# Windowed attention and two feed-forward layers on one core: wider token groups, a shorter first attention, paired later attention, weights converted in place

## The chip, the cores and the metric

The program runs on one core of a Trainium2 chip. The metric is the device time of the program in microseconds (us), lower is better. TensorE does the matmuls (PE in the profile, PEld is its loading of weights), VectorE is DVE, ScalarE is ACT, GpSimd is POOL, and SP issues all DMAs.

## The reference, cut to what matters

All values are float32. There are 4 sequences of 576 tokens, 8 heads of 64, so 2304 tokens of 512 columns between the stages.

```python
# attention: a token sees itself and the 63 tokens before it
scores = scale * q @ k.T;  scores = where(0 <= rel < 64, scores, -1e9)
attn = exp(scores - max(scores)); attn = attn / (sum(attn) + 1e-9); x = attn @ v
# first layer: 512 -> 2048 -> 512
h = x @ w_in;  g = h * tanh(softplus(h));  x = g @ w_out
# second layer: 512 -> 1024 -> 512
h = x @ w_in2; sm = softmax(h); solu = h * sm
ln = (solu - mean(solu)) / sqrt(var(solu) + 1e-6) * g_ln
out = ln @ w_out2
```

## The kernel before, in words

Every matmul of the two layers is made of three: an operand is split into a high part `hi`, which holds its leading bits, and a rest `lo`, and hi x lo, lo x hi and hi x hi are added in PSUM.

**Weights.** They arrive as 64-bit words, two 32-bit halves to a value, in 48 pieces of 128 x 512 values (512 KB each). `convert` (L816) makes the steps of one piece. `c_load` (L304) fetches it into one of 3 `st` buffers; the first four go into a room of their own (`room_b`). `c_up` (L322) scales the upper halves into a new tile `wf`, on ACT (the first two pieces also on POOL). `c_low` (L332) scales the lower halves into a tile `wl`, on POOL. `c_bits` (L338, the instruction is L340) and `c_sign` (L344, L346) join them bit by bit in `wf`, on DVE. `c_hi` rounds `wf` to the high part (L263 on ACT, L267 on DVE) and `c_lo` subtracts it (L281 on POOL, L283 on DVE). 16 pieces each belong to `w_in` and `w_out`, 8 each to `w_in2` and `w_out2`.

**Attention.** It goes by blocks of 64 tokens, 36 in all, four matmuls of two heads each. The first group's 6 blocks come before anything else: scores in PSUM (L439, with the mask added by L442), maximum (L451), four exponentials with sums (L459), `a_norm` (L498, L499), the multiplication on POOL (L504), transposes (L518), a copy (L275), the product with v (L541), and its split into hi (`a_x`, L275) and lo (`a_xl`, L562), which lie in the group's tile `xt`. The other 30 blocks (`attend`, L913) are issued two at a time between the matmuls of the first layer. Each block has its own passes: scale and mask (L469), maximum (L475), subtraction (L481) and sum (L493) on DVE; only the exponentials (L489) of two blocks stand together, as they need another activation table than the first layer's function. Scores, transposes and products use the PSUM ring `a` of two buffers of one bank each; the first 6 blocks use the banks of `x2` and `h`.

**First layer.** There are 6 groups of 384 tokens. A tile of work is one group and one of 16 chunks of 128 columns of the 2048: `pe_m1` (L574, matmul L587, 12 of them), the activation (L597), rounding (L263 or L267) and rest (L283), then `pe_m2` (L621, 8 matmuls) and `pe_m2l` (L632, 4), which add into four banks `x2`. Groups 0 and 1 take chunks 0 to 7 in turn, write a partial sum to memory, and then chunks 8 to 15, where the partial sum is added; the other groups take all 16 at once. The m2 of a tile comes some tiles behind its m1 (`LAG`). At a group's end four copies (L657, L659) or sums (L647) go out to memory.

**Second layer.** 18 tiles of 128 tokens: load, split (L701), rest (L706 on POOL), 24 matmuls of 512 columns (L715), maximum (L722), exponential (L728), the product and statistics (L734 to L744), the power on POOL (L750), normalising (L756), transposes (L763), hi and lo (L769, L773), 24 matmuls (L788), copy (L795) and store.

**What sets the order.** Each function above is a step with a cost per engine and a due time. `Schedule.run` (L98) keeps a clock for every engine, takes the step that can start first (among those within `PATIENCE` the one with the earliest due time), picks the engine where `COSTS` names several, and issues the instructions in that order. So the order on each engine, and on SP for the DMAs, is fixed before the program runs, by modelled costs; on the chip semaphores hold an engine back where an input is late. Buffers are rings with a fixed number of places (`sch.run(dict(...))` at the end).

Of the kernel before, what the change touches and what calls it, by code (L numbers as in the profile page):

```python
# [26 lines left out]
LD = 2  # L27
CUT = 8
# [11 lines left out]
    "g_hi": {"dve": 0.28, "act": 0.42}, "g_lo": {"dve": 0.48},  # L40
    "x2": {"act": 0.39, "dve": 0.5},
# [15 lines left out]
G_AT = 10.0
K0_LATER = -3.349
W_STEP = 5.115
M4_LATER = -0.753  # L60
# [118 lines left out]
def attention_moe_solu(  # L179
# [27 lines left out]
    GROUPS = [384] * 6  # L207
# [3 lines left out]
    N0 = GROUPS[0] // BLK  # L211
    assert N0 <= NBB
    GMAX = max(GROUPS)

# [34 lines left out]
    st_p = actx.enter_context(tc.tile_pool(name="st", bufs=3))  # L249
# [8 lines left out]
    ps_a = tctx.enter_context(tc.tile_pool(name="ps_a", bufs=2, space=PSUM, side="right"))  # L258
# [62 lines left out]

    def c_up(e, p):  # L322
        p["wf"] = st_p.tile([P, 512], F32, tag="wf", name="wf")
        w = p["st"][:, :, 1].bitcast(F32)
        if e == "act":
            nc.scalar.activation(out=p["wf"], in_=w, func=ACTF.Copy, scale=2.0**-112)  # L326
        else:
            nc.gpsimd.tensor_scalar(
                out=p["wf"], in0=w, scalar1=2.0**-112, scalar2=0.0, op0=ALU.mult, op1=ALU.add
            )  # L330

    def c_low(p):  # L332
        p["wl"] = st_p.tile([P, 512], U32, tag="wl", name="wl", bufs=2)
        nc.gpsimd.tensor_scalar(  # L334
            out=p["wl"], in0=p["st"][:, :, 0], scalar1=0.9325 * 2.0**-29, scalar2=0.0, op0=ALU.mult, op1=ALU.add
        )

    def c_bits(p):  # L338
        wb = p["wf"].bitcast(U32)
        nc.vector.scalar_tensor_tensor(  # L340
            out=wb, in0=wb, scalar=3, in1=p["wl"], op0=ALU.logical_shift_left, op1=ALU.bitwise_or
        )

    def c_sign(p):  # L344
        wb = p["wf"].bitcast(U32)
        nc.vector.scalar_tensor_tensor(  # L346
            out=wb, in0=p["st"][:, :, 1], scalar=0x80000000, in1=wb, op0=ALU.bitwise_and, op1=ALU.bitwise_or
        )

# [32 lines left out]
    NI = NF * NG  # L382
    needs += [NI - NF + 4 + W_STEP * (n + 1) for n in range(2 * KD + NF2)]
# [21 lines left out]
    def open_q0():  # L405
        room["q"] = wpool.tile([P, N0 + 1, NP, P], F32, tag="w1", name="room_q")
        room["r"] = room["q"][:, N0, :2].bitcast(BF16)

# [25 lines left out]
    def a_qk(n):  # L434
        ps = ps_a.tile([P, NP, P], F32, tag="a", name="ps_s")
        r = room["r"]
        for p in range(NP):
            early = n < N0
            nc.tensor.matmul(out=ps[:, p, :], lhsT=qt[n][:, p, :], rhs=kt[n][:, p, :], start=True, stop=not early)  # L439
            if early:  # L440

                nc.tensor.matmul(  # L442
                    out=ps[:, p, :], lhsT=r[:, 0, :P], rhs=r[:, 0, P:] if n == 0 else r[:, 1, :P], start=False, stop=True
                )
# [11 lines left out]
    def a_exp0(n, ps=range(4)):  # L456
        s, nm, su, w = s_t[n]
        for p in ps:
            nc.scalar.activation(  # L459
                out=s[:, p], in_=w[:, p], func=ACTF.Exp, scale=scale, bias=nm[:, p:p + 1], accum_out=su[:, p:p + 1]  # L460
            )
        if 3 in ps:
            s_t[n] = s, nm, su

    def a_scale(n):
        ps = s_t[n]
        s = at_p.tile([P, NP, P], F32, tag="s", name="s", bufs=4)
        m = (mask_0 if n % NBB == 0 else mask_n).unsqueeze(1).to_broadcast([P, NP, P])
        nc.vector.scalar_tensor_tensor(out=s, in0=ps, scalar=scale, in1=m, op0=ALU.mult, op1=ALU.add)  # L469
        s_t[n] = s  # L470

    def a_max(n):
        s = s_t[n]
        nm = sm_p.tile([P, NP], F32, tag="nm", name="nm")
        nc.vector.tensor_reduce(out=nm, in_=s, axis=AX.X, op=ALU.max, negate=True)  # L475
        su = sm_p.tile([P, NP], F32, tag="su", name="su")
        s_t[n] = (s, nm, su)

    def a_sub(n):
# [34 lines left out]
    def a_tr(n):
        s = s_t.pop(n)
        ps = bank("x2", n, "ps_t", NP, P)
        for p in range(NP):
            nc.tensor.transpose(ps[:, p, :], s[:, p, :], ident)  # L518
        pt_t[n] = ps

    def a_pt(e, n):
        pt = at_p.tile([P, NP, P], F32, tag="pt", name="pt", bufs=2)
        copy(e, pt, pt_t[n])
        pt_t[n] = pt
# [10 lines left out]
    def a_pv(n):  # L535
        pt = pt_t.pop(n)
        ps = bank("h", n, "ps_o", NP, BLK)
        for p in range(NP):
            for h in range(2):
                r = slice(h * BLK, (h + 1) * BLK)  # L540
                nc.tensor.matmul(  # L541
                    out=ps[r, p, :],
                    lhsT=vt[n][:, (2 * p + h) * D:(2 * p + h + 1) * D],
                    rhs=pt[:, p, r],
                    start=True, stop=True,
                )
        x_t[n] = ps

    def a_x(e, n):
# [4 lines left out]
        hi = xt[j][:, 0, :, o:o + BLK]  # L554
        lo = xt[j][:, 1, :, o:o + BLK]
# [10 lines left out]

    its = [(j, f) for fs in (range(CUT), range(CUT, NF)) for j in range(2) for f in fs]
    its += [(j, f) for j in range(2, NG) for f in range(NF)]
    opens = {i for i, (j, f) in enumerate(its) if f == 0 or (f == CUT and j < 2)}
    closes = {i for i, (j, f) in enumerate(its) if f == NF - 1 or (f == CUT - 1 and j < 2)}  # L570
# [3 lines left out]
    def pe_m1(i):  # L574
        j, f = its[i]
        n = GROUPS[j]
# [4 lines left out]
        assert all(b in x_done for b in range(starts[j] // BLK, (starts[j] + GROUPS[j]) // BLK))  # L581
# [4 lines left out]
        for idx, (k, a, b) in enumerate(terms):  # L586
            nc.tensor.matmul(  # L587
                out=ps[:, :n], lhsT=w[:, a, k, fs], rhs=x[:, b, k, :n],
# [5 lines left out]
    def act_m(i):  # L594
        n = GROUPS[its[i][0]]
        c = m_p.tile([P, GMAX], F32, tag="mc", name="mc", bufs=3)
# [3 lines left out]
    def g_h(e, i):  # L600
        n = GROUPS[its[i][0]]
# [4 lines left out]
    def g_l(e, i):  # L606
        n = GROUPS[its[i][0]]
# [3 lines left out]
    def pe_m2(i):  # L611
        j, f = its[i]
        n = GROUPS[j]
# [5 lines left out]
        for m in range(KD):  # L619
            for a in (0, 1):  # L620
                nc.tensor.matmul(  # L621
                    out=acc[j][m][:, :n], lhsT=w[:, a, f % 4, m * P:(m + 1) * P], rhs=g[:, 0, :n],
# [3 lines left out]
    def pe_m2l(i):  # L626
        j, f = its[i]
        n = GROUPS[j]
        g = gt.pop(i)
        w = wt["w2", f // 4]  # L630
        for m in range(KD):
            nc.tensor.matmul(  # L632
                out=acc[j][m][:, :n], lhsT=w[:, 0, f % 4, m * P:(m + 1) * P], rhs=g[:, 1, :n],
# [9 lines left out]
    def evac_part(i, m):  # L643
        j, f = its[i]
# [7 lines left out]
    def evac_x2(e, i, m):  # L652
        j, f = its[i]
# [8 lines left out]
    def store_x2(i, m):  # L662
        j, f = its[i]
# [3 lines left out]
    with tc.manual_schedule():  # L667
        NI = len(its)
# [29 lines left out]
        def b_split(t):  # L698
            r = xr.pop(t)
            xs[t] = B["x"].tile([P, 2, KD, P], F32R, tag="xs", name="xs", bufs=3)  # L700
# [115 lines left out]
        def convert(p):  # L816
# [268 lines left out]
```

## Time and profile before

| | |
|---|---|
| median of 3 runs | 740.83 us (740.2 to 741.36) |
| profiled execution | 740.77 us |
| its span, first to last instruction | 739.0 us |
| mean granted TensorE clock | 0.988 |
| busy: PE, PEld, DVE, ACT, POOL | 706.6, 653.2, 425.4, 295.8, 156.3 us |
| moved by DMA | 70.45 MB |

Busy time is the length of all instructions of an engine without double counting. The matmul times are modelled at their end, so a batch's price is best read from the start of one batch to the start of the next. In a row of the groups, the mean is one instruction's length, and instructions that follow each other overlap by some tens of nanoseconds.

### The profile page before, as it was taken

What the parts mean: (1) busy time and instruction counts of PE and PEld (TensorE: products, weight loads), DVE (VectorE), ACT (ScalarE), POOL (GpSimd) and SP (SyncE); (2) the same over time, 40 slices, a digit from 0 to 9 for tenths busy, and PEclk for the clock granted to TensorE, in tenths of its full rate; (3) what the DMA queues carried; (4) which work ended last, traced back from release to release, by engine and by line L of the source; (5) the groups of instructions that cost most, each with busy time, mean ns of one, the idle gap of its engine ahead of it and who ended that gap; (6) DMA issues with size and microseconds to landing.
All of it is one profiled execution on the core that took longest, in us unless ns stands there. A gap on an engine that the chain in (4) does not pass through costs nothing.

```text
span 739.0 us, 11115 instructions
## 1 busy us (share of the span) xinstructions
PE 706.6 (96%) x4344; PEld 653.2 (88%) x4344; DVE 425.4 (58%) x734; ACT 295.8 (40%) x551; POOL 156.3 (21%) x176
## 2 busy tenths in 40 slices
PE   6797889699999999999999999999999999999998
PEld 5696789699999999999999999999888888888886
DVE  3999999955645334424434412676575646464642
ACT  4665435454454345334434433345432323232221
POOL 3556644421111011011101110331122111121000
PEclk9899999899999999999999999999999999999999
DMA  8645565652622201302222011331111111111001
GB/s 299 243 155 196 163 213 173 192 178 98 192 83 100 86 30 58 129 29 75 69 88 70 1 44 58 114 114 58 59 43 57 43 43 43 43 44 43 29 16 43
DMA packets 42916, 70.45 MB, mean 95 GB/s; under 512 B 3312, under 2 KB 27376, under 8 KB 42864
## 3 DMA queue, kind: packets, MB, share of 16 engines
q1 hardware_dynamic: 42864, 69.75, 28.6%
q8 instruction: 34, 0.56, 0.3%
q14 instruction: 18, 0.15, 0.1%
HBM read 58.72 MB, written 11.01 MB: 94 GB/s over the span
## 4 chain that ended last, share of the span: by engine, by line
PE 85%; DVE 10%; issue 2%; ACT 1%; DMA 1%; POOL 0%; SPq 0%; DVEq 0%; ACTq 0%; POOLq 0%
PE ps_h L587 24%; PE x L621 16%; PE h L715 14%; PE po L788 13%; PE x L632 8%; PE ps_s L439 4%; DVE wf L346 3%; DVE wf L340 3%; PE pt L763 2%; PE ps_o L541 2%; PE ps_t L518 2%; DVE g L283 1%; DVE w L267 1%; DMA room_q<-qk 0%; DVE su L493 0%
## 5 line engine op out<-in xcount | busy, mean ns | idle before, releaser
L587 PE MATMUL ps_h<-xt,w 128*128 128x384 f32 x1152 | 221.5, 341 | 5.6 <-POOL w L281 2.0
L587 PEld LDWEIGHTS ps_h<-xt,w 128*128 128x128 f32 x1152 | 204.5, 191 | 8.3 <-POOL w L281 2.8
L621 PE MATMUL x<-g,w 128*128 128x384 f32 x768 | 153.5, 340 | 9.4 <-ACT xs L657 6.2
L621 PEld LDWEIGHTS x<-g,w 128*128 128x128 f32 x768 | 134.9, 190 | 12.0 <-ACT xs L657 6.9
L283 DVE SCALAR_TENSOR_TENSOR g<-mc,g 128x384 fp32r<-128x384 f32 x96 | 69.8, 728 | 109.2 <-ACT g L263 108.5
L597 ACT ACTIVATE mc<-ps_h 128x384 f32<-128x384 f32 x96 | 47.0, 490 | 154.9 <-PE ps_h L587 154.6
L715 PE MATMUL h<-w,xs 128*128 128x512 f32 x432 | 104.2, 396 | 0.4 <-DVE y L734 0.4
L788 PE MATMUL po<-w,lz 128*128 128x512 f32 x432 | 102.3, 393 | 0.0
L715 PEld LDWEIGHTS h<-w,xs 128*128 128x128 f32 x432 | 80.8, 188 | 19.6 <-PE x L632 0.7
L504 POOL TENSOR_TENSOR s<-s,rs 128x512 f32<-128x512 f32 x36 | 40.6, 1145 | 257.3 <-DVE rs L498 109.7
L788 PEld LDWEIGHTS po<-w,lz 128*128 128x128 f32 x432 | 80.0, 188 | 16.4
L632 PE MATMUL x<-g,w 128*128 128x384 f32 x384 | 84.1, 340 | 0.0
L632 PEld LDWEIGHTS x<-g,w 128*128 128x128 f32 x384 | 67.6, 189 | 0.7
L334 POOL TENSOR_SCALAR wl<-st 128x512 uint32<-128x512 uint32 x44 | 37.6, 855 | 63.5 <-DMA st<-w_in 20.1
L722 DVE TENSOR_REDUCE nm<-h 128x1 f32<-128x1024 f32 x18 | 22.0, 1224 | 49.1 <-PE h L715 49.1
L263 ACT ACTIVATE g<-mc 128x384 fp32r<-128x384 f32 x87 | 45.8, 526 | 4.9 <-PE x L632 2.2
L326 ACT ACTIVATE wf<-st 128x512 f32<-128x512 f32 x44 | 29.3, 672 | 45.3 <-DMA st<-w_in 21.0
L706 POOL TENSOR_TENSOR xs<-xr,xs 128x512 fp32r<-128x512 f32 x18 | 23.3, 1294 | 95.2 <-ACT xs L701 95.2
L281 POOL TENSOR_TENSOR w<-wf,w 128x512 fp32r<-128x512 f32 x22 | 33.1, 1510 | 43.9 <-DVE w L267 40.3
L346 DVE SCALAR_TENSOR_TENSOR wf<-st,wf 128x512 uint32<-128x512 uint32 x44 | 40.5, 921 | 1.2
L340 DVE SCALAR_TENSOR_TENSOR wf<-wf,wl 128x512 uint32<-128x512 uint32 x48 | 40.8, 851 | 0.1
L701 ACT ACTIVATE xs<-xr 128x512 fp32r<-128x512 f32 x18 | 11.4, 632 | 62.9 <-PE h L715 46.9
(75 smaller groups left out, 671.9 us busy)
## 6 DMA issues: line engine op xcount, KB each, us to landing
qk<-qk SPq DMA_DIRECT2D x30, 512.0 KB, 4.4
st<-w_out SPq DMA_DIRECT2D x24, 512.0 KB, 3.6
st<-w_in SPq DMA_DIRECT2D x20, 512.0 KB, 3.8
v<-v SPq DMA_DIRECT2D x30, 256.0 KB, 2.8
x2d<-xs SPq DMA_DIRECT2D x24, 192.0 KB, 2.1
xr<-x2d SPq DMA_DIRECT2D x18, 256.0 KB, 3.1
out<-o SPq DMA_DIRECT2D x18, 256.0 KB, 2.0
room_b<-w_in SPq DMA_DIRECT2D x4, 512.0 KB, 7.8
```

Source lines behind the costliest of these rows:

```text
L263: nc.scalar.activation(out=hi, in_=x, func=ACTF.Copy, scale=1.0 if g is None else g)
L283: nc.vector.scalar_tensor_tensor(out=lo, in0=x, scalar=1.0 if g is None else g, in1=hi.bitcast(F32), op0=ALU.mult, op1=ALU.subtract)
L334: nc.gpsimd.tensor_scalar(out=p["wl"], in0=p["st"][:, :, 0], scalar1=0.9325 * 2.0**-29, scalar2=0.0, op0=ALU.mult, op1=ALU.add)
L340: nc.vector.scalar_tensor_tensor(out=wb, in0=wb, scalar=3, in1=p["wl"], op0=ALU.logical_shift_left, op1=ALU.bitwise_or)
L346: nc.vector.scalar_tensor_tensor(out=wb, in0=p["st"][:, :, 1], scalar=0x80000000, in1=wb, op0=ALU.bitwise_and, op1=ALU.bitwise_or)
L504: nc.gpsimd.tensor_tensor(out=s, in0=s, in1=rs.to_broadcast([P, NP, P]), op=ALU.mult)
L587: nc.tensor.matmul(out=ps[:, :n], lhsT=w[:, a, k, fs], rhs=x[:, b, k, :n], start=(idx == 0), stop=(idx == len(terms) - 1),)
L597: nc.scalar.activation(out=c[:, :n], in_=ht.pop(i)[:, :n], func=ACTF.Mish)
L621: nc.tensor.matmul(out=acc[j][m][:, :n], lhsT=w[:, a, f % 4, m * P:(m + 1) * P], rhs=g[:, 0, :n], start=(i in opens and a == 0), stop=False,)
L632: nc.tensor.matmul(out=acc[j][m][:, :n], lhsT=w[:, 0, f % 4, m * P:(m + 1) * P], rhs=g[:, 1, :n], start=False, stop=i in closes,)
L715: nc.tensor.matmul(out=h2[t][:, c, :], lhsT=x[:, a, k, :], rhs=wt["w3", c][:, b, k, :], start=(idx == 0), stop=(idx == len(terms) - 1),)
L788: nc.tensor.matmul(out=po[t], lhsT=lz[:, a, f, :], rhs=wt["w4", f // 4][:, b, f % 4, :], start=(c == 0 and idx == 0), stop=(c == 2 and idx ...
```

## The change: what it does

- The groups are 512, 512, 512, 384 and 384 tokens. The first four chunks of group 0 are done in two halves of 256 tokens, first all four of tokens 0 to 255, then of 256 to 511. There are 84 tiles: 8 of 256, 44 of 512, 32 of 384.
- Only 4 blocks, half a group, come before the first layer. Their scores lie in the `x2` banks, their exponentials in a spare part of the q room. The 28 others come in 14 pairs; a pair is one tile of 1024 columns for each pass (L465 to L520 before), and the ring `a` has one buffer of two banks. The transposed values are copied back over the exponentials in two halves. The multiplication may go to POOL or DVE.
- `c_up` and `c_low` write in place, into the staged piece; both run on ACT (the lower half of the first two pieces on POOL, the upper on either). Bits and sign are joined in the lower halves. `c_hi` runs on ACT, `c_lo` on DVE; the tiles `wf` and `wl` are gone, and there are 4 staging buffers.
- The activation's tile has 2 places instead of 3, the second layer's split input 2 instead of 3.
- Due times and modelled costs are new; positions are counted in time (`pos`), not in tiles.

```diff
 COSTS = {
-    "up0": {"act": 0.57, "pool": 0.846}, "up": {"act": 0.57},
-    "pt0": {"act": 0.5}, "x0": {"act": 0.29}, "pt": {"act": 0.5}, "x": {"act": 0.29},
-    "w0_hi": {"dve": 0.36, "act": 0.51}, "w0_lo": {"dve": 0.63, "pool": 1.5},
-    "w_hi": {"act": 0.51, "dve": 0.36}, "w_lo": {"dve": 0.63, "pool": 1.5},
+    "up0": {"act": 0.58, "pool": 0.7}, "up": {"act": 0.58},
+    "pt0": {"act": 0.5, "dve": 0.68}, "x0": {"act": 0.29}, "pt": {"act": 0.5}, "x": {"act": 0.5},
+    "low0": {"pool": 0.83}, "low": {"act": 0.58},
+    "w0_hi": {"dve": 0.43, "act": 0.54}, "w0_lo": {"dve": 0.69},
+    "w_hi": {"act": 0.54}, "w_lo": {"dve": 0.69},
...
+    "mul0": {"pool": 1.05, "dve": 0.69}, "mul": {"pool": 2.2, "dve": 1.23},
...
-    GROUPS = [384] * 6
+    GROUPS = [512, 512, 512, 384, 384]
...
-    N0 = GROUPS[0] // BLK
+    N0 = GROUPS[0] // BLK // 2
...
-    st_p = actx.enter_context(tc.tile_pool(name="st", bufs=3))
+    st_p = actx.enter_context(tc.tile_pool(name="st", bufs=4))
...
-    ps_a = tctx.enter_context(tc.tile_pool(name="ps_a", bufs=2, space=PSUM, side="right"))
+    ps_a = tctx.enter_context(tc.tile_pool(name="ps_a", bufs=1, space=PSUM, side="right"))
...
     def c_up(e, p):
-        p["wf"] = st_p.tile([P, 512], F32, tag="wf", name="wf")
         w = p["st"][:, :, 1].bitcast(F32)
         if e == "act":
-            nc.scalar.activation(out=p["wf"], in_=w, func=ACTF.Copy, scale=2.0**-112)
+            nc.scalar.activation(out=w, in_=w, func=ACTF.Copy, scale=2.0**-112)
...
+    def c_low(e, p):
+        w = p["st"][:, :, 0]
+        if e == "act":
+            nc.scalar.activation(out=w, in_=w, func=ACTF.Copy, scale=0.9325 * 2.0**-29)
...
+        lw, uw = p["st"][:, :, 0], p["st"][:, :, 1]
         nc.vector.scalar_tensor_tensor(
-            out=wb, in0=wb, scalar=3, in1=p["wl"], op0=ALU.logical_shift_left, op1=ALU.bitwise_or
+            out=lw, in0=uw, scalar=3, in1=lw, op0=ALU.logical_shift_left, op1=ALU.bitwise_or
         )
...
+    n = GROUPS[0] // 2
+    its = [(0, f, o, o + n) for o in (0, n) for f in range(HALF)]
+    its += [(0, f, 0, 2 * n) for f in range(HALF, CUT)]
+    its += [(1, f, 0, GROUPS[1]) for f in range(CUT)]
+    its += [(j, f, 0, GROUPS[j]) for j in range(2) for f in range(CUT, NF)]
+    its += [(j, f, 0, GROUPS[j]) for j in range(2, NG) for f in range(NF)]
...
     def a_scale(n):
         ps = s_t[n]
-        s = at_p.tile([P, NP, P], F32, tag="s", name="s", bufs=4)
+        s = at_p.tile([P, 2 * NP, P], F32, tag="s2", name="s", bufs=2)
...
+            qk = step(dict(pe=1.75), t + offs[0], a_qk, n, after=lks + pv_last[-2:-1], new=[S], uses=ks + [S])
+            sc = step(dict(dve=1.23), t + offs[1], a_scale, n, after=[qk, masks], new=[s], uses=[S, s])
+            mx = step(dict(dve=1.2), t + offs[2], a_max, n, after=[sc], new=[nm], uses=[s, nm])
...
+                su = step(dict(dve=1.23), t + offs[3], a_sub, n, after=[mx], uses=[s, nm])
+                ex = step(dict(act=1.03 + 2.66), t + offs[4], a_exp, n, after=[su], uses=[s])
+                sm = step(dict(dve=1.2), t + offs[5], a_sum, n, after=[ex], uses=[s])
...
+            mu = step(COSTS["mul"], t + offs[6], a_mul, n, after=[r], uses=[s, rs])
+            tr = step(dict(pe=0.87), t + offs[7], a_tr, n, after=[mu] + pv_last[-1:], new=[T], uses=[s, T])
+            c0 = step(COSTS["pt"], t + offs[8], a_pt, n, 0, after=[tr], uses=[T, s])
+            c1 = step(COSTS["pt"], t + offs[8], a_pt, n, 1, after=[tr, c0], uses=[T, s])
...
-            w1=4, w2=4, st=3, wf=3, wl=2, qk=LD, v=LD, a=2, s=4, nm=4, rs=4, pt=2, x2=4, h=2, xt=2, mc=3,
-            g=LAG, xs=4, bxr=1, bxs=3, b0=1, b1=1, bnm=4, bsu=4, by=2, bst=4, bt=1, blz=2, bo=2, bot=2,
+            w1=4, w2=4, st=4, qk=LD, v=LD, a=1, s=3, nm=4, rs=4, s2=2, nm2=4, rs2=4, x2=4, h=2, xt=2, mc=2,
+            g=LAG, xs=4, bxr=1, bxs=2, b0=1, b1=1, bnm=4, bsu=4, by=2, bst=4, bt=1, blz=2, bo=2, bot=2,
```

## Rows read from the trace of the kernel before

**Rows 1.** Page, busy tenths in 40 slices of 18.5 us.
```profile
PE   6797889699999999999999999999999999999998
...
DVE  3999999955645334424434412676575646464642
```

**Rows 2.** Busy us (instructions) by stage; then clock, DMA share, GB/s.
```profile
0.00:20.00 20.00, 13.19 (x107) 11.22 (x108) 8.32 (x21) 10.39 (x41) 7.97 (x21) 1.00 0.91 305
...
32.96:155.00 122.04, 105.32 (x639) 98.83 (x640) 117.62 (x167) 58.45 (x103) 62.37 (x56) 0.94 0.55 178
...
155.00:515.40 360.40, 360.40 (x2468) 355.73 (x2467) 163.63 (x303) 154.38 (x268) 44.61 (x42) 1.00 0.25 81
...
515.40:739.00 223.60, 219.57 (x1032) 180.93 (x1031) 123.66 (x222) 64.43 (x114) 33.54 (x51) 1.00 0.13 42
```

**Rows 3.** Chain of waits in order of time: start, length, what.
```profile
102.82 2.08 PE ps_h L587 x12
...
106.98 2.08 PE ps_h L587 x12
...
150.83 1.78 PE ps_s L439 x16
...
568.12 5.60 PE h L715 x24
574.59 5.48 PE po L788 x24
```

**Rows 4.** Timeline of PE: start, length, instructions, idle time before and its releaser.
```profile
140.50 1.65 PE L621 MATMUL x<-g,w 128*128 128x384 f32 x4 [4.41 <-ACT xs L657]
...
179.68 1.03 PE L518 MATMUL ps_t<-ident,s 128*128 128x128 f32 x8
...
180.47 1.65 PE L621 MATMUL x<-g,w 128*128 128x384 f32 x8
...
183.86 0.69 PE L541 MATMUL ps_o<-pt,v 128*64 128x64 f32 x16
```

**Rows 5.** Timeline of DVE, the fourth and the sixth block's L562.
```profile
26.70 0.42 DVE L562 TENSOR_TENSOR xt<-ps_o,xt 128x256 fp32r<-128x256 f32 x1
...
32.48 0.42 DVE L562 TENSOR_TENSOR xt<-ps_o,xt 128x256 fp32r<-128x256 f32 x1 [0.59 <-ACT xt L275]
```

**Rows 6.** Groups by line from 32.96 to 155 us: busy, mean, idle before.
```profile
L346 DVE SCALAR_TENSOR_TENSOR wf<-st,wf 128x512 uint32<-128x512 uint32 x31 | 30.8, 993 | 0.8
```

**Rows 7.** Groups by line of DVE, whole span.
```profile
L283 DVE SCALAR_TENSOR_TENSOR g<-mc,g 128x384 fp32r<-128x384 f32 x96 | 69.8, 728 | 109.2 <-ACT g L263 108.5
...
L722 DVE TENSOR_REDUCE nm<-h 128x1 f32<-128x1024 f32 x18 | 22.0, 1224 | 49.1 <-PE h L715 49.1
L734 DVE TENSOR_TENSOR y<-h,y 128x1024 f32<-128x1024 f32 x18 | 21.9, 1215 | 2.0 <-ACT y L728 2.0
...
L499 DVE RECIPROCAL rs<-rs 128x4 f32<-128x4 f32 x36 | 6.4, 178 | 1.2
...
L346 DVE SCALAR_TENSOR_TENSOR wf<-room_b,wf 128x512 uint32<-128x512 uint32 x4 | 2.7, 686 | 0.1
```

**Rows 8.** Groups by line of ACT, whole span.
```profile
L597 ACT ACTIVATE mc<-ps_h 128x384 f32<-128x384 f32 x96 | 47.0, 490 | 154.9 <-PE ps_h L587 154.6
...
L326 ACT ACTIVATE wf<-st 128x512 f32<-128x512 f32 x44 | 29.3, 672 | 45.3 <-DMA st<-w_in 21.0 <-DMA st<-w_out 19.4 <-DVE g L283 2.4
...
L275 ACT ACTIVATE pt<-ps_t 128x512 f32<-128x512 f32 x36 | 20.2, 596 | 9.9 <-PE ps_t L518 9.9
L728 ACT ACTIVATE y<-h,nm 128x1024 f32<-128x1024 f32 x18 | 20.2, 1122 | 8.2 <-DVE nm L722 8.2
...
L263 ACT ACTIVATE w<-wf 128x512 fp32r<-128x512 f32 x7 | 4.4, 634 | 4.5 <-DVE wf L346 4.5
```

**Rows 9.** Timeline of ACT around one switch of tables.
```profile
52.52 1.28 ACT L489 ACT_TABLE_LOAD   x1
53.82 1.15 ACT L489 ACTIVATE s<-s 128x512 f32<-128x512 f32 x2
```

More of the change, by code (lines that the diff above doesn't have):

```diff
@@ L434, in a_qk @@
     def a_qk(n):
[L435 to L444, printed above, removed]
+        early = n < N0
+        ns = (n,) if early else (n, n + 1)
+        if early:
+            ps = ps_x2.tile([P, NP, P], F32, tag="x2", name="ps_s")
+        else:
+            ps = ps_a.tile([P, 2 * NP, P], F32, tag="a", name="ps_s")
+        r = room["r"] if early else None
+        for c, m in enumerate(ns):
+            for p in range(NP):
+                o = ps[:, c * NP + p, :]
+                nc.tensor.matmul(out=o, lhsT=qt[m][:, p, :], rhs=kt[m][:, p, :], start=True, stop=not early)
+                if early:
+                    nc.tensor.matmul(
+                        out=o, lhsT=r[:, 0, :P], rhs=r[:, 0, P:] if n == 0 else r[:, 1, :P], start=False, stop=True
+                    )
         s_t[n] = ps
@@ L536, in a_pv @@
         pt = pt_t.pop(n)
[L537 to L546, printed above, removed]
+        if n < N0:
+            ps, ns = ps_h.tile([P, NP, BLK], F32, tag="h", name="ps_o"), (n,)
+        else:
+            ps, ns = ps_a.tile([P, NP, 2 * BLK], F32, tag="a", name="ps_o"), (n, n + 1)
+        for c, m in enumerate(ns):
+            for p in range(NP):
+                for h in range(2):
+                    r = slice(h * BLK, (h + 1) * BLK)
+                    nc.tensor.matmul(
+                        out=ps[r, p, c * BLK:(c + 1) * BLK],
+                        lhsT=vt[m][:, (2 * p + h) * D:(2 * p + h + 1) * D],
+                        rhs=pt[:, c * NP + p, r],
+                        start=True, stop=True,
+                    )
         x_t[n] = ps
@@ L580, in pe_m1 @@
         assert ("w1", 0, f) in split_done
-        assert all(b in x_done for b in range(starts[j] // BLK, (starts[j] + GROUPS[j]) // BLK))
+        assert all(b in x_done for b in range((starts[j] + a0) // BLK, (starts[j] + a1) // BLK))
         w = wt["w1", f // 4]
@@ L890, in values @@
[L890 to L901 removed]
+            w, pt = bufs
@@ L902, in values @@
+            pv = step(dict(pe=0.648 * len(cps)), t + offs[0], a_pv, n, after=cps, new=[O], uses=[pt, O] + w)
             new = []
@@ L926, in mish @@
         def mish(i):
-            j, f = its[i]
-            k = GROUPS[j] / 384
+            j, f, a0, a1 = its[i]
+            k = (a1 - a0) / 384
+            pe = pe_of(i)
             h, mc, g = (Buf(x) for x in ("x2" if i in H_X2 else "h", "mc", "g"))
-            o = [i + x for x in MISH_AT]
+            o = [pos[i] + x for x in MISH_AT]
             m1 = step(
-                dict(pe=2.081 * k), o[0], pe_m1, i, after=x_of[j] + [split_of["w1", 0, f]], new=[h],
+                dict(pe=pe / 2), o[0], pe_m1, i, after=list({id(x_of[n]): x_of[n] for n in range((starts[j] + a0) // BLK, (starts[j] + a1) // BLK)}.values()) + [split_of["w1", 0, f]] + ([m1_of[i - 1]] if i else []), new=[h],
@@ L938, in mish @@
+            gl = step(COSTS["g_lo" if a1 - a0 > 256 else "g_lo0"], o[3], g_l, i, after=[gh], uses=[mc, g])
             new = []
```

382 lines of the change are left out of this document (201 added, 181 removed).

## The prediction, made before the result was known

> **What bounds the kernel now.** I read the 40 slices first, then a table of stages, then the chain of waits. The slices [rows 1] show two regimes: up to slice 9 (about 150 us) DVE stands at 9 nearly throughout and PE at 5 to 9; from then on PE stands at 9 to the last slice and DVE mostly at 2 to 7. The stages say it in numbers [rows 2]. From 32.96 (first matmul of the feed-forward) to 155 us DVE is busy 117.62 of 122.04 us and PE 105.32; from 155 to 515.4 PE is busy 360.40 of 360.40; from 515.4 to the end 219.57 of 223.60. So the opening is DVE's and the rest is TensorE's.
>
> The chain [rows 3] gives TensorE's prices. One column tile of 384 tokens is 24 matmuls: 12 of m1, 8 of m2 and 4 of m2l, from 102.82 to 106.98 = 4.16 us (0.173 us each). A 512-wide batch of 24 takes 5.60 us (L715) or 5.48 (L788). A pair of attention blocks takes 1.78 for the scores, 0.79 for the transposes (from 179.68 to 180.47) and twice 0.69 for the values [rows 3, 4]: 3.9 us.
>
> These terms give the span back. First m1 at 32.96; 96 tiles x 4.16 = 399.4; the 30 blocks that remain = 15 pairs x 3.9 = 58.5; last part 739.0 - 515.4 = 223.6. Together 714.5; the span is 739.0, so 24.5 us are lost to waits and to the half clock after them. All of it lies before 155 us, since behind that PE is always busy. The profiled execution took 740.77 us, 1.77 over its span, and the median of the runs is 740.83: the sum below is made on the span, and 1.8 are added.
>
> **The change, part by part.**
>
> *Wider groups.* After: 8 tiles of 256 tokens, 12 + 32 = 44 of 512 and 32 of 384. For a 512 tile I take m1 at L715's price and m2 at L788's: (5.60 + 5.48)/2 = 5.54 us. A 256 tile has no row; on the line through 4.16 and 5.54 it is 2.78. Sum: 44 x 5.54 + 8 x 2.78 + 32 x 4.16 = 243.8 + 22.2 + 133.1 = 399.1 us, against 399.4. The width itself gives nothing: the same columns cross the array, and the small price per matmul that is saved is lost to the halves and to the 512 price. Ends: 5.48 and 5.60 for the 512 tile move the sum by 2.6 us either way; a 256 tile at 4.16 (no gain from being shorter) adds 11 us, one at 24 x 0.111 = 2.67 (the 128-wide score matmuls, 1.78/16) takes off 0.9. The line is kept, since the 128-wide row lies below it too.
>
> *Four blocks, not six, before the first m1.* The subtraction that ends a block's share of x is L562. It starts at 26.70 for the fourth block and at 32.48 for the sixth [rows 5]; m1 follows 0.06 us after its end. Left as it is, m1 would start at 27.1 us instead of 32.96. Five loads of 256 KB also go (two of q, one of k, two of v); the first 20 us move 305 GB/s [rows 2], so 1.31 MB are 4.3 us of the queue. Ends 22.8 and 27.1 (above: 31, if the in-place conversion comes late); I take 25.0. The two blocks move into the 28 that run beside the matmuls: 14 pairs x 3.9 = 54.6, which is 3.9 us less PE time after the start.
>
> *Conversion in place.* Each of 48 pieces is two scalings, two bit operations, hi and lo. Before, POOL did one scaling and part of the lo's, and DVE part of the hi's. After, ACT has both scalings and nearly all hi's, DVE the bit operations and lo's, POOL two pieces. What DVE wins is in the rows: L346 costs 0.993 us in the opening, beside POOL, and 0.686 on the staged pieces [rows 6, 7]. With POOL nearly gone from conversion I take 0.69 for each of three operations, 2.07 us a piece. The writes now step over every second word; reads of that form cost ACT 0.672 (L326) [rows 8], and I take the same for the writes (ends: 0.634, a dense one (L263), and double). The four staging buffers hold a piece until its lo is done; four pieces in flight against one needed every 5 us leave room.
>
> *Later attention in pairs.* DVE: four passes over 1024 columns at 1.22 (L722, L734), two tiny ones like L499 at 0.18, and a subtraction of 512 columns, 0.69 as L346: 5.9 us a pair. ACT: two table loads of 1.28, one exponential of 1024 at 1.12 (L728), three 512-wide copies at 0.60 (L275): 5.5 us [rows 7 to 9]. The multiplication may stand on POOL or, at 1.22, on DVE.
>
> The load of L489 lasts 1.28 us and the exponential starts 1.30 us after the load's start, so here nothing stands between them [rows 9]; a switch is costed at the load alone. The Trainium skill, page "ScalarE: Activation LUTs", section "What ACT_TABLE_LOAD costs", speaks against that: it puts every switch of sets at 2.66 us, since a drain of 1.38 follows the load, and by it the twelve switches of the opening would cost ACT an estimated 16 us more. Our row shows no such drain.
>
> *The new opening.* It reaches to the first tile of group 1, the 13th. By then these must be done: 16 pieces, 6 pairs (group 0's second half and group 1) and 12 tiles.
> - PE without a wait: 25.0 + 8 x 2.78 + 4 x 5.54 + 6 x 3.9 = 93 us.
> - DVE: 8.3 for the first blocks (its busy time in the first 20 us) + 16 x 2.07 + 6 x 5.9 + 12 x 0.73 (L283) = 86 us [rows 2, 7].
> - ACT: 10.4 + 16 x (2 x 0.672 + 0.634) + 6 x 5.5 + 12 x 2 x 0.49 (L597, and as much for a rounding) = 87 us [rows 2, 8].
>
> Before, DVE alone was the limit and was packed to 96%. Now two engines carry nearly the same load and every pair and piece passes from one to the other, so I take 90% packing from 8 us on: 8 + 87/0.9 = 105. PE then waits 12 us; with 2 for the half clock after waits, S = 14. The end of the opening is what counts: an m1 earlier than 25 only lengthens the wait. Ends: 96% gives 99 and S = 6, with nothing for the clock; 75% gives 124 and S = 33; the six muls on DVE (93 us) give 111 and S = 20. Behind the opening, DVE needs some 16 x 2.07 + 4 x 5.9 + 24 x 0.73 = 74 us over 24 tiles x 5.54 + 4 x 3.9 = 149 us of PE, so the conversion of the second half of the weights, which before still held PE up to 143 us (a wait of 4.41 us at 140.50 [rows 4]), is covered.
>
> *The rest.* The last part keeps its instructions; with two input buffers instead of three there are still 12 us between the end of one L715 batch and the need for the next but one, against a load, split and subtraction of some 5 us. I cost it at 0 (ends: -1 and +4).
>
> Sum: 25.0 + 399.1 + 54.6 + 14 + 223.6 = 716.3 of span, 718.1 us of time; before minus after is 8.0 (start) + 0.3 + 3.9 + 10.5 (waits) = 22.7.
>
> **Rivals.**
> - *The two engines pack as well as DVE did alone* (S = 6), and the 512 tile costs 5.48: 718.1 - 8 - 2.6 = 707 us. For it: ACT is busy only 58.45 of 122.04 us in the old opening, so load moves to an engine that was half free. Against: a pair is one chain over four engines, and each of its links is twice as long as a block's.
> - *ACT and DVE hand each other the wait* (75%, S = 33): 737 us. For it: ACT's order is fixed, and a copy out of PSUM that PE needs can now stand behind three conversions (2 us) or two table loads with an exponential (3.7 us). Against: DVE was in the same place for PE before, and its 96% left no such holes.
> - *A table switch costs its length once more*, 1.28 us on ACT for each of twelve: 8 + (87 + 15)/0.9 = 122, S = 31, 735 us. The Trainium skill's page named above is for it; the row of L489 [rows 9] is against it.
> - *One PSUM tile for all later attention: slower.* The ring of two one-bank buffers becomes one of two banks, which scores, transposes and values of a pair use in turn. If the planner's order leaves nothing to put between, PE stands through the scaling pass (1.22) and two copies (1.20) of each pair: 2.4 x 14 = 34 us, 752. It decides from 1.6 us a pair (22.7/14). Against: with two buffers PE waited in none of the 12 pairs after 155 us, and a pair has some 22 us there (four tiles of 5.54).
> - *It does not do what it says*: halves cost what 384 does (+8 with the 5.48), m1 starts at 31 (+6) and PE waits as before (S = 22): 740, no change.
>
> **How the numbers follow.** Forecast (710 to 728) 0.47, well packed 0.18, hand-over 0.18, table switch 0.02, PSUM slower 0.12, no change 0.03. The time is the forecast's, 718. The range, 703 to 738, takes in the first three cases with 4 us below 707, and leaves out the last two. A measurement here tells 0.2% (1.5 us) from no change: faster 0.85, same 0.03, slower 0.12.
>
> **What would show it.** First m1 matmul at 23 to 27 us; 12 m1 of 512 columns in 2.7 to 2.8 us; DVE and ACT both above 85% busy from the start to about 105 us and below 60% after; bit operations at 0.69; last part of 223 us. The forecast is wrong if PE has repeated gaps of 1 to 2 us in front of transposes or values after the opening, if the wide tiles cost over 5.8 us, or if the first m1 comes after 30 us.

## The result and the profile after

The changed kernel takes 720.98 us (median, 720.77 to 722.02), the kernel before beside it 740.52 (739.93 to 741.36): a ratio of 0.9738, 95% interval 0.9721 to 0.9755. The prediction was 718, between 703 and 738. The time came out right; of the steps behind it some did not, and their errors offset each other.

The profiled execution has a span of 719.1 us (before 739.0). Its 40 slices of 18.0 us:

```profile
PE   6669999999999999999999999999999999999997
...
DVE  4998897886164143442453314666665555555552
ACT  4688788876235233443442524564233232323221
```

Against [rows 1], PE reaches 9 in the fourth slice and stays there until the last one; DVE is at 8 or 9 from the second slice to the sixth (108 us), at 7 or 8 to the ninth, and at 6 or less from then on. The stages follow: busy us (instructions) of PE, PEld, DVE, ACT, POOL, then clock, DMA share, GB/s. They are cut at the first m1 (31.84) and at the first m1 of the 13th tile (108.09).

```profile
20.00:31.84 11.84, 6.28 (x44) 5.04 (x44) 11.57 (x21) 7.54 (x18) 3.17 (x3) 0.80 0.94 349
31.84:60.00 28.16, 21.06 (x205) 19.68 (x205) 27.08 (x40) 20.69 (x36) 3.80 (x2) 0.96 0.39 129
60.00:108.09 48.09, 46.12 (x382) 39.79 (x382) 41.56 (x60) 41.03 (x65) 3.80 (x2) 1.00 0.55 181
...
108.09:491.28 383.19, 383.19 (x2241) 340.95 (x2242) 181.53 (x263) 181.63 (x288) 2.57 (x2) 1.00 0.31 103
491.28:719.10 227.82, 223.57 (x1057) 185.15 (x1055) 124.77 (x223) 65.83 (x115) 34.90 (x52) 1.00 0.13 42
```

Before, DVE was packed until 155 us [rows 2]; now it is packed only to 60 us (27.08 of 28.16). From 60 to 108 it is busy 86% and ACT 85%, and PE 96%. From 108.09 on PE is never idle before the last part, while DVE and ACT are each busy 47%. The waits of PE in the opening (line, releaser, us in total, times, longest), then its only one in the stage from 108.09 to 491 us, which ends as that stage begins:

```profile
PE ps_h L658 <- DVE xt L636: 3.2, 1, 3.2
PE ps_s L486 <- DVE xt L636: 1.8, 1, 1.8
PE ps_h L658 <- DVE w L290: 1.6, 2, 1.1
PE ps_o L614 <- ACT s L282: 1.5, 1, 1.5
PE ps_t L579 <- DVE s L532: 0.5, 1, 0.5
```

```profile
PE ps_h L658 <- DVE xt L636: 0.4, 1, 0.4
```

All but one are released by DVE. PE's timeline (start, length, instructions, idle time before) shows the start, a 256-wide tile (12, 8 and 4 matmuls: from 64.69 to 67.57, 2.88 us) and the first m1 of the 13th tile:

```profile
27.10 1.06 PE L579 MATMUL ps_t<-ident,room_q 128*128 128x128 f32 x4 [3.99 <-DVE rs L561]
28.85 1.12 PE L614 MATMUL ps_o<-room_q,room_kv 128*64 128x64 f32 x16 [0.69 <-ACT room_q L282]
...
31.84 0.58 PE L658 MATMUL ps_h<-xt,w 128*128 128x256 f32 x1
...
64.69 1.60 PE L658 MATMUL ps_h<-xt,w 128*128 128x256 f32 x12
66.13 1.12 PE L692 MATMUL x<-g,w 128*128 128x256 f32 x8
67.09 0.64 PE L703 MATMUL x<-g,w 128*128 128x256 f32 x4
67.57 1.60 PE L658 MATMUL ps_h<-xt,w 128*128 128x256 f32 x12
...
108.09 2.11 PE L658 MATMUL ps_h<-xt,w 128*128 128x512 f32 x8 [0.44 <-DVE xt L636]
```

### The profile page after: what moved, and what is told of

Same layout as the page of the kernel before. It is cut to its first block, busy times and chain, and to the rows that moved or that the text cites. A ratio compares the mean times of both kernels' runs of the same rounds, so it can differ in the third digit from the quotient of the medians.

```text
span 719.1 us, 10096 instructions
## 1 busy us (share of the span) xinstructions
PE 693.6 (96%) x4048; PEld 602.5 (84%) x4048; DVE 395.4 (55%) x622; ACT 325.8 (45%) x554; POOL 54.1 (8%) x78
## 4 chain that ended last, share of the span: by engine, by line
PE 89%; DVE 4%; ACT 4%; DMA 2%; issue 1%; SPq 0%; ACTq 0%
PE ps_h L658 25%; PE x L692 17%; PE h L785 14%; PE po L858 14%; PE x L703 8%; PE ps_s L486 4%; PE ps_o L614 2%; PE pt L833 2%; PE ps_t L579 2%; DMA st<-w_out 1%; ACT L668 1%; DVE w L290 1%; DVE g L290 1%; DMA st<-w_in 1%; DVE st L355 1%
## 5 line engine op out<-in xcount | busy, mean ns | idle before, releaser
L658 PE MATMUL ps_h<-xt,w 128*128 128x512 f32 (+2 forms) x1008 | 213.7, 361 | 5.2 <-DVE xt L636 3.6
L658 PEld LDWEIGHTS ps_h<-xt,w 128*128 128x128 f32 x1008 | 178.6, 189 | 27.8 <-DVE xt L636 4.6
L692 PE MATMUL x<-g,w 128*128 128x512 f32 (+2 forms) x672 | 148.6, 362 | 0.0
L290 DVE SCALAR_TENSOR_TENSOR g<-mc,g 128x512 fp32r<-128x512 f32 (+2 forms) x84 | 53.9, 642 | 154.4 <-ACT g L270 144.2
L668 ACT ACTIVATE mc<-ps_h 128x512 f32<-128x512 f32 (+2 forms) x84 | 45.1, 537 | 139.9 <-PE ps_h L658 138.7
L703 PE MATMUL x<-g,w 128*128 128x512 f32 (+2 forms) x336 | 81.0, 362 | 0.0
L270 ACT ACTIVATE g<-mc 128x512 fp32r<-128x512 f32 (+2 forms) x74 | 42.7, 578 | 13.5 <-PE x L703 11.7
L334 ACT ACTIVATE st<-st 128x512 f32<-128x512 f32 x44 | 29.8, 678 | 17.4 <-DMA st<-w_out 9.5
L486 PE MATMUL ps_s<-qk 128*128 128x128 f32 x256 | 31.6, 276 | 2.7 <-DVE xt L636 1.8
L486 PEld LDWEIGHTS ps_s<-qk 128*128 128x128 f32 x256 | 30.7, 191 | 3.8 <-DVE xt L636 2.0
L349 DVE SCALAR_TENSOR_TENSOR st<-st 128x512 uint32<-128x512 uint32 x44 | 30.3, 688 | 6.2 <-ACT st L341 6.0
```

What stands on the lines that cost most here:

```text
L270: nc.scalar.activation(out=hi, in_=x, func=ACTF.Copy, scale=1.0 if g is None else g)
L290: nc.vector.scalar_tensor_tensor(out=lo, in0=x, scalar=1.0 if g is None else g, in1=hi.bitcast(F32), op0=ALU.mult, op1=ALU.subtract)
L334: nc.scalar.activation(out=w, in_=w, func=ACTF.Copy, scale=2.0**-112)
L349: nc.vector.scalar_tensor_tensor(out=lw, in0=uw, scalar=3, in1=lw, op0=ALU.logical_shift_left, op1=ALU.bitwise_or)
L486: nc.tensor.matmul(out=o, lhsT=qt[m][:, p, :], rhs=kt[m][:, p, :], start=True, stop=not early)
L658: nc.tensor.matmul(out=ps[:, :n], lhsT=w[:, a, k, fs], rhs=x[:, b, k, a0:a1], start=(idx == 0), stop=(idx == len(terms) - 1),)
```

## The experiments

Each time stands with its ratio to the kernel before, timed beside it on the same chip, and the ratio's 95% interval. The changed kernel's ratio, 0.9738, is the one to hold a ratio against: the kernel before itself took between 740.06 and 741.13 us (medians), so differences of times carry up to 1 us of that. A profile shows one execution out of four, and not always a middle one. The planner works out each engine's order from costs. Where an edit leaves all costs alone, order and buffers stay as they are, and what the edit does is measured, with the granted clock that comes of it; where a cost changes, the whole order is planned anew. That difference turned out to be the main thing to watch.

**Is the opening bound by DVE or by ACT?** One operation taken off each, the order kept. The sign step of the first 16 pieces (DVE), so that the kernel leaves out the sign of these weights:

```diff
-        nc.vector.scalar_tensor_tensor(out=lw, in0=uw, scalar=0x80000000, in1=lw, ...)
+        if p["i"] >= 16:
+            nc.vector.scalar_tensor_tensor(out=lw, in0=uw, scalar=0x80000000, in1=lw, ...)
```

> The changed kernel with the order of every engine kept, but without the sign step (L355, 0.69 us on DVE) of the first 16 weight pieces, so these weights have no sign. Eight of the sixteen lie before 60 us. Theory A (until 60 us PE waits for DVE alone, behind that PE is its own limit): the 5.5 us of DVE work before 60 us come off, 714 to 717 us. Theory B (the forecast's: DVE and ACT limit the opening alike, and either alone brings half): 718 to 720.

717.06 us, 0.9679 (0.9664 to 0.9694): 4 us off the change's time, at the upper end of the first theory's 714 to 717. The stage from 31.84 to 60 us has 21.59 us of DVE instead of 27.08, and PE 23.51 instead of 21.06:

```profile
31.84:60.00 28.16, 23.51 (x214) 22.24 (x214) 21.59 (x35) 22.52 (x39) 3.79 (x2) 0.90 0.51 164
```

The scaling of the lower halves of pieces 2 to 15 (ACT), with a zero of one column read in its place, so that the kernel leaves out the last three bits of these weights:

```diff
-            nc.scalar.activation(out=w, in_=w, func=ACTF.Copy, scale=0.9325 * 2.0**-29)
+            if p["i"] >= 16:
+                nc.scalar.activation(out=w, in_=w, func=ACTF.Copy, scale=0.9325 * 2.0**-29)
```

> The changed kernel with its order kept, but without ACT's scaling of the lower halves (L341, 0.69 us) of pieces 2 to 15; the join takes a zero in their place, so the last three bits of these weights are missing. ACT has some 9 us less to do in the opening, 4.5 of it before 60 us. Theory A (DVE alone): 720 to 721.5, at most 1 us gained. Theory B (ACT and DVE alike): 716 to 718.

720.19 us, 0.9723 (0.9706 to 0.9740): an operation of the same length (0.686 us) taken from ACT gives about 1 us, which the intervals do not tell from nothing. So here DVE's operations lie on the path, and ACT's, as far as these runs tell, beside it.

**What does POOL cost DVE?** The same scalings put on POOL, order kept (`if e == "act":` becomes `if False:`):

> The changed kernel, order kept, with the scaling of the lower halves on POOL, as before the change, for all 48 pieces. Theory A, with DVE's two-input operations held up while POOL reads: the bit operations of the opening rise from 0.69 to 0.8 or 0.9 us, and 2 to 5 us are lost, 723 to 726. Theory B (ACT is a limit too, and POOL takes work off it): 716 to 719, with the bit operations at 0.7.

723.19 us, 0.9759 (0.9743 to 0.9776): +2.2 us by the medians, 1.6 by the ratios, whose intervals overlap. By groups of lines from 20 to 108.09 us (busy, mean ns), first the change, then this kernel:

```profile
L355 DVE SCALAR_TENSOR_TENSOR st<-st 128x512 uint32<-128x512 uint32 x15 | 10.4, 691 | 0.3
L349 DVE SCALAR_TENSOR_TENSOR st<-st 128x512 uint32<-128x512 uint32 x15 | 10.3, 687 | 0.0
```

```profile
L349 DVE SCALAR_TENSOR_TENSOR st<-st 128x512 uint32<-128x512 uint32 x14 | 10.9, 781 | 0.0
...
L355 DVE SCALAR_TENSOR_TENSOR st<-st 128x512 uint32<-128x512 uint32 x13 | 9.7, 749 | 0.3
```

ACT is relieved, and DVE's bit operations take 8 to 14% longer (0.75 and 0.78 us, a little less than the first theory's 0.8 to 0.9; the time is within its range). The loss need not be all theirs: the granted clock from 31.84 to 60 us is 0.74 here, 0.96 in the changed kernel.

**The conversion alone**, in the kernel before (groups of 384, six first blocks, single blocks kept):

```diff
+    "low0": {"pool": 0.83}, "low": {"act": 0.58},
-    "w_hi": {"act": 0.51, "dve": 0.36}, "w_lo": {"dve": 0.63, "pool": 1.5},
+    "w_hi": {"act": 0.54}, "w_lo": {"dve": 0.69},
...
-    st_p = actx.enter_context(tc.tile_pool(name="st", bufs=3))
+    st_p = actx.enter_context(tc.tile_pool(name="st", bufs=4))
...
-            nc.scalar.activation(out=p["wf"], in_=w, func=ACTF.Copy, scale=2.0**-112)
+            nc.scalar.activation(out=w, in_=w, func=ACTF.Copy, scale=2.0**-112)
...
```

> The kernel before with one part of the change: conversion in place, both scalings and the rounding on ACT, the rest on DVE, four staging buffers; groups of 384, six blocks first, single blocks and all due times as before. The order is planned anew. If the opening's DVE load is what the change removes, some 20 of DVE's 118 us between 33 and 155 us go, and the time comes to 726 to 731 (about half of the change's 20 us). If the new tiles and the shorter first attention bring it, 737 to 741.

722.53 us, 0.9759 (0.9738 to 0.9781): 18.6 us faster than before, better than either expected. The intervals of this ratio and the change's overlap: all the rest of the change is worth 1.6 us by the medians, which these runs can't tell from nothing. (The rest takes in the change's own due times, as this kernel keeps those of before.) Its profile shows an execution of 725.18 us, the longest of its four. From its first m1 (31.14) to 155 us, to be held against the second of [rows 2], and from 155 to 515:

```profile
31.14:155.00 123.86, 115.47 (x750) 112.24 (x752) 104.97 (x181) 95.78 (x169) 10.85 (x8) 0.96 0.59 188
155.00:515.00 360.00, 359.52 (x2426) 352.97 (x2427) 156.88 (x298) 164.05 (x284) 29.65 (x28) 1.00 0.24 80
```

DVE's load falls from 117.62 us to 104.97 in nearly the same stretch, ACT's rises from 58.45 to 95.78, POOL's falls from 62.37 to 10.85, and PE does 115.47 us instead of 105.32. One more thing is different: in this opening ACT hardly waits for weights to arrive. Its waits from 31 to 155 us, in the kernel before and in the conversion alone:

```profile
ACT wf L326 <- DMA st<-w_in: 17.1, 12, 3.1
ACT wf L326 <- DMA st<-w_out: 15.6, 11, 3.8
```

```profile
ACT st L326 <- DMA st<-w_in: 3.5, 5, 1.1
```

**Which part of the conversion?** One part of it put back at a time, each planned anew. Lower halves on POOL (`"low": {"pool": 0.588}`):

> E4 with one part put back: the scaling of the lower halves on POOL at its old modelled cost; planned anew. By what it cost in the changed kernel (E3, 2.2 us): 724 to 727. If POOL's part in the conversion is what E4's 18 us come from: 730 or more.

727.67 us, 0.9826 (0.9811 to 0.9840): 5.1 over the conversion alone. Its bit operations rise from 715 and 714 ns to 782 and 756, now beside 32 scalings on POOL of 800. The time lies between the two expectations.

The lo's on POOL or DVE (`"w_lo": {"dve": 0.63, "pool": 1.5}`; the planner put 31 on POOL, 27 of them from 20 to 155 us):

> E4 with one part put back: the lo subtraction may go to POOL (1.50 us) or DVE, at the old modelled costs; planned anew, which puts most of the lo's on POOL. POOL's two-input work in front of DVE's, and weights that come 0.8 us later: 728 to 736. By E5 (half of them on POOL, 0.8 us lost): 723 to 725.

723.24 us, 0.9772 (0.9756 to 0.9788): 0.7 over it, no difference that the intervals tell. DVE loses 27 operations of 0.7 us in that stretch, and pays with bit operations of 921 and 807 ns (groups by line, 20 to 155 us):

```profile
L282 POOL TENSOR_TENSOR w<-st,w 128x512 fp32r<-128x512 f32 x24 | 36.3, 1521 | 46.0 <-ACT w L264 46.0
...
L341 DVE SCALAR_TENSOR_TENSOR st<-st 128x512 uint32<-128x512 uint32 x32 | 29.5, 921 | 9.8 <-ACT st L333 5.0 <-issue 3.5 <-POOL w L282 1.3
L347 DVE SCALAR_TENSOR_TENSOR st<-st 128x512 uint32<-128x512 uint32 x32 | 25.8, 807 | 0.8
```

The hi's on ACT or DVE (`"w_hi": {"act": 0.51, "dve": 0.36}`; 23 on DVE):

> E4 with one part put back: the rounding to hi may go to DVE (0.36 us modelled) or ACT; planned anew. Before, DVE did 25 of them in the opening at 0.61 us, 15 of its 118 us. If DVE's amount of work sets the opening: 728 to 735. If not: 722 to 726.

725.53 us, 0.9799 (0.9777 to 0.9822): 3.0 over it. From 31.14 to 155 us DVE is busy 113.02 us, 8 more than in the conversion alone, and the time still lies where it was expected if DVE's amount of work does not set the opening. At that price (3.0 us for 8) the 12.7 us that the conversion takes off DVE would be worth some 5 us of its 18.6, an estimate. Together the three make 8.8 of the 18.6 us. The other 10 are not assigned: they may lie in the parts acting together, in the staging buffers, in the costs that the planner is told, or in the order that it makes of them. All three variants keep the four staging buffers, and in all three ACT waits only 3 to 9 us for weights from 31 to 155 us, against 32.7 before; no run changes the number of buffers by itself.

The same on the changed kernel with the order kept, every other lo of the first 32 pieces on POOL:

```diff
-        rest(e, lo, w, hi, p["g"])
+        rest("pool" if p["i"] < 32 and p["i"] % 2 else e, lo, w, hi, p["g"])
```

> The changed kernel, order kept, with the lo subtraction of every second one of the first 32 pieces on POOL (1.50 us there by the rows of before, 0.69 on DVE). Before the change 22 of 48 stood on POOL. Theory A (DVE binds the opening, and POOL's two-input work holds DVE up for about its own length and makes PE wait for the weights): DVE gains 16 x 0.69 and loses more in its other operations, 725 to 732. Theory C (only the amount of DVE work counts, not where POOL reads): 716 to 719.

721.75 us, 0.9750 (0.9736 to 0.9765), +0.8: neither expectation. L355 goes from 691 to 913 ns and L349 from 687 to 760; the operations that DVE sheds and the length that it gains nearly cancel: from 20 to 108.09 us it is busy 77.9 us instead of 80.2.

**A shorter DVE chain in three late pairs**, order kept: for three pairs the subtraction and the sum leave DVE, and ACT takes them over in its exponentials (bias and accumulation per 128 columns).

```diff
+    FOLD = (4, 6, 8)
...
+        if n in FOLD:
+            a_neg(n)
+            a_exp1(n, range(2 * NP))
+            return
```

> The changed kernel, order kept, but for the first three pairs (blocks 4 to 9) the subtraction of the maximum and the sum (two DVE passes of 1.22 us) are done by ACT inside the exponential: eight exponentials of 128 columns with a bias and a running sum, some 2.8 us instead of 1.06. DVE has 7.3 us less before 60 us, ACT 5 us more. Theory A (DVE alone binds until 60 us): 714 to 718. Theory B (both bind alike): 719 to 723.

720.46 us, 0.9724 (0.9707 to 0.9740): the same, as the second theory expected. DVE has only 18.71 us in 31.84 to 60, and still PE waits, and its clock there is 0.82. The stage, and the chain of waits inside it:

```profile
31.84:60.00 28.16, 21.95 (x187) 20.78 (x185) 18.71 (x33) 23.57 (x63) 3.79 (x2) 0.82 0.38 125
```

```profile
46.42 1.28 ACT L520
...
47.71 1.99 ACT s L520 x10
...
49.95 0.96 ACT s L520 x5
50.90 0.49 ACT xt L282
...
51.41 0.70 DVE xt L646
...
52.16 2.93 PE ps_h L668 x12
```

The chain has moved to ACT. Taking an operation off DVE paid (no sign step: 4 us); handing these two to ACT did not: DVE binds, and ACT is close behind.

**An earlier m1** at the cost of later pairs, planned anew: `BESIDE_AT` begins with (1.2, 1.5) in place of (5.205, 3.072).

> The changed kernel with the due times of the first two pairs four units (17 us) later, so that the first four blocks and the first weights come ahead of them; the order is planned anew. The prediction's statement, that an earlier first m1 only lengthens the wait, since the opening's end is set by the other engines' work: first m1 at 25 to 28 us instead of 31.84, time within 2 us of 721. Rival, that the start counts: 715 to 718.

730.42 us, 0.9874 (0.9860 to 0.9889), both missed. m1 starts at 29.75, two us earlier, and then PE waits 6.2 us for DVE's weights:

```profile
PE x L692 <- DVE w L290: 6.2, 2, 4.7
...
PE ps_t L579 <- DVE s L568: 3.9, 1, 3.9
```

The clock of the stage from 31.84 to 60 is 0.69 in place of 0.96. It fits "an m1 earlier than 25 only lengthens the wait", but as the whole order differs it does not show it.

**Narrower groups**, planned anew: `GROUPS = [512, 384, 384, 384, 384, 256]` in place of `[512, 512, 512, 384, 384]`.

> The changed kernel with groups of 512, 384, 384, 384, 384 and 256 tokens: 24 tiles of 256, 12 of 512 and 64 of 384. By the measured 2.88, 5.46 and 4.16 us a tile that is 69.1 + 65.5 + 266.2 = 400.8 us against 23.0 + 240.2 + 133.1 = 396.3 for the change, so 724 to 727 if the width counts only by these prices. If the wide tiles bring the gain in another way (fewer activations and roundings on ACT and DVE), 732 or more.

725.99 us, 0.9808 (0.9790 to 0.9827): +5.0, where the prices of the tiles gave 4.5. It agrees with them, but as the whole order differs it does not show them.

**The multiplication** on POOL or DVE in the conversion alone (`"mul": {"pool": 1.05, "dve": 0.69}`), planned anew:

> E4 (the kernel before with the conversion in place alone, 722.5 us) and one more edit: the attention's multiplication may go to DVE (0.69 us) or POOL (1.05) instead of POOL alone; planned anew. In E4 PE waited 10.0 us in 6 places for that multiplication on POOL, which takes 1.38 us in the opening. If the waits are POOL's length, 714 to 719, better than both kernels; if they are only the end of a chain that DVE sets, 721 to 725.

730.16 us, 0.9862 (0.9847 to 0.9876): 7.6 us slower, though the waits behind POOL were to go (in the conversion alone 10.0 us in six, the first line of its waits):

```profile
PE ps_t L520 <- POOL s L506: 10.0, 6, 4.1
```

All but 1.0 us of them went, but the first m1 came at 35.41 instead of 31.14, and the clock from 20 to 60 us was 0.84 instead of 0.92. With the earlier m1 above (9.4 us) this is the second case in which an edit that was to gain or to cost nothing lost 7 to 9 us once the order was planned anew, more than any single part of the conversion that was put back. How much of that is the edit's and how much the order's was not separated.

## Why the prediction was right, step by step

**What bounds.** Right: the opening was DVE's, and nearly all of the gain lies there. At the prices measured, the 19.9 us of span are: start 1.1, tiles 2 to 4, attention -1, and so 16 to 18 for waits, half clock and what else is lost in the opening. Forecast were 8.0, 0.3, 3.9 and 10.5, together 22.7. The sum is 3 us off, its terms up to 7: that the time was met is partly luck.

**First m1.** Missed: 25.0 forecast, 31.84 measured, beyond the 30 us that the forecast named as its own limit. The prediction took two blocks' work away and left the rest in place; but the planner put work of two late pairs and of the weights ahead of the fourth block on DVE. That block's maximum (L498) starts at 20.01 us; before (L451) it started at 14.96. DVE's timeline before L636:

```profile
24.73 1.21 DVE L554 TENSOR_REDUCE su<-s 128x8 f32<-128x1024 f32 x1
25.86 0.16 DVE L561 TENSOR_SCALAR rs<-su 128x4 f32<-128x4 f32 x1
...
27.19 1.17 DVE L532 SCALAR_TENSOR_TENSOR s<-ps_s,mask_n 128x1024 f32<-128x1024 f32 x1
28.28 1.59 DVE L355 SCALAR_TENSOR_TENSOR room_b<-room_b 128x512 uint32<-128x512 uint32 x1
...
30.25 1.21 DVE L538 TENSOR_REDUCE nm<-s 128x8 f32<-128x1024 f32 x1
31.37 0.41 DVE L636 TENSOR_TENSOR xt<-ps_o,xt 128x256 fp32r<-128x256 f32 x1
```

The three pair passes shown are 3.6 us, and three more lie between 14.95 and 20.09. The L355 of 1.59 us instead of 0.69 lies beside a multiplication of POOL (27.42 to 29.32). PE's transposes wait 3.99 us for L561. The pairs are not all of the miss: with the first two pairs due later (an earlier m1, above) m1 still came only at 29.75.

**Opening.** Its end was forecast at 105, 107 with the clock; the 13th tile's m1 starts at 108.09. S was forecast at 14, and 14 us are lost: the 76.25 us from the first m1 to there hold matmuls worth about 62 us at the full-clock prices, PE is idle for 9.07 us (67.18 busy), and the other 5 us are matmuls dearer than those prices, of which the clock of 0.96 until 60 us makes about 1. That S agrees is partly luck: the start came 6.8 us later, and 62 us of matmuls stood where 68 were forecast. That both engines carry nearly the same load, 86 and 87 us, failed: DVE is busy 80.2 of the 88.1 us from 20 to 108.09 (91%), ACT 69.3 (79%), and ACT is at 64 and 73% until 60 us and at 85 only then. The runs without the sign step and without the lower scaling say the same: DVE's operations count, ACT's hardly. The end of the opening came 1 to 3 us behind the forecast though its start came 6.8 late; no run isolates what the late start cost.

**Attention.** The prediction and the section on the change miscounted: of 36 blocks 4 come first, so 32 remain, in 16 pairs and not 28 in 14. The page shows it in the loads of the late blocks (queue, form, count, KB, us):

```profile
qk<-qk SPq DMA_DIRECT2D x32, 512.0 KB, 5.3
```

By the right count, 16 x 3.9 = 62.4 us stand where 54.6 were forecast. A pair is cheaper than taken: 1.70 for the scores (from 54.32 to 56.02), 0.79 for the transposes and 1.08 for both values together (from 308.19 to 309.27 below), 3.6 us. Sixteen are 57, of which 4 come before the first m1: 53. The two errors nearly cancel. But the kernel before pays the same prices: its 15 pairs are 54 us, of which 2 come before its first m1. So the attention costs 1 us more than before, where the prediction had it 3.9 us cheaper.

```profile
303.57 1.03 PE L579 MATMUL ps_t<-ident,s 128*128 128x128 f32 x8
304.36 1.17 PE L703 MATMUL x<-g,w 128*128 128x512 f32 x4
...
308.19 1.15 PE L614 MATMUL ps_o<-s,v 128*64 128x64 f32 x32
309.27 2.11 PE L692 MATMUL x<-g,w 128*128 128x512 f32 x8
```

**Tiles.** Where nothing slows it, a 512 tile takes 5.44 us (forecast 5.54), a 256 tile 2.88 (2.78); the sum is then 395.5 for 399.1. On average the 512 tiles are dearer: the 383.19 us from 108.09 to 491 us hold 40 of them, 30 tiles' worth of 384 and ten pairs, which leaves about 5.54 for each, just what was forecast; by the same count a 384 tile took 4.2 before. "The width itself gives nothing" was a little too low: the tiles together are 2 (by these averages) to 4 us (by the shortest prices) cheaper. The narrower groups agree with 5.0 us. One pair more than before takes back part of what the width gives.

**Conversion.** 0.69 for each bit operation was exact (687 and 691 ns), and the in-place scaling on ACT close (685 ns, 0.672 taken). The third operation, the subtraction for lo, took 0.80 us, not 0.69. Nor did four staging buffers "leave room": from 40 to 108 us the loads of weights wait 28.7 us for a lo to set one free. The lo's from 20 to 108.09 us, and that wait of the DMA queue:

```profile
L290 DVE SCALAR_TENSOR_TENSOR w<-st,w 128x512 fp32r<-128x512 f32 x13 | 10.0, 797 | 0.4 <-ACT w L270 0.4
```

```profile
SPq L326 <- DVE w L290: 28.7, 11, 6.4
```

The weights of the second half held PE nowhere.

**The rivals.** One two-bank buffer for all late attention, slower from 1.6 us a pair, did not occur: after the opening PE's whole wait is 0.4 us. In the opening it showed twice, in the 1.8 us that scores (L486) and the 0.5 us that transposes (L579) wait for DVE to empty that buffer. A table switch costs its load: the exponential starts 1.29 us after the load's start, as in [rows 9].

```profile
45.97 1.28 ACT L549 ACT_TABLE_LOAD   x1
47.26 1.06 ACT L549 ACTIVATE s<-s 128x1024 f32<-128x1024 f32 x1
```

"Halves cost what 384 does, m1 at 31, PE waits as before" was right in its second part alone. **The rest**: the last part's price is as before; its window is 227.82 instead of 223.60 because m2 of four tiles, not two, lies behind its first batch (less 2.08 for each: 219.5 and 219.4). The prediction counts the m2 of two tiles twice, in its 96 tiles and in its 223.6; it does so in both sums, so the difference does not change.

Not settled: how 10 of the 18.6 us of the conversion divide, and what the fourth staging buffer has in them. No version tried that computes the whole result beat the changed kernel by more than the intervals.

## What to carry to other kernels

Price the stage that binds, engine by engine, and ask first which single operations leave the engine that holds it: one part of this change alone gave nearly all of the gain, and the wider tiles, the shorter start and the pairs together were within the uncertainty of the rest. Where a planner sets the order, a moved operation moves many others; take or shift one operation with the order kept to learn its price, and count on several us from a new plan (here twice 7 to 9, to the slower side). Count the blocks before you price them.

## What the runs showed of the hardware

- DVE's operations on two inputs stretch when POOL works beside them: 0.69 us alone, 0.75 to 0.78 beside POOL scalings, 0.76 to 0.91 beside POOL subtractions in the changed kernel (0.81 to 0.92 in the conversion alone). Moving an operation of 0.69 to POOL may then free nothing.
- At the full granted clock (1.00) the fp32r matmul costs 5.44/24 = 227 ns at 512 columns, 4.16/24 = 173 at 384 and 2.88/24 = 120 at 256: 0.44, 0.45 and 0.47 ns a column, so narrow tiles cost a few per cent.
- ACT reading and writing every second word takes 0.685 us for 512 columns in the opening; writing dense ones it takes 0.67 to 0.68 where it reads every second word, and 0.63 where it reads dense ones too.
